# An SSM-and-MLP mix on one core: three parameter rows behind three first blocks, transposes reordered, sine and cosine moved, and no joining block

## The chip, the cores and the metric

The kernel runs on one core of one Trainium2 chip. A core has a matrix engine (PE, whose weight loads are shown as PEld), a vector engine (DVE, VectorE), an activation engine (ACT, ScalarE), a general engine (POOL, GpSimd) and a sequencer for transfers (SP, SyncE). Each runs its own list of instructions in order; semaphores tie the lists together. SP and ACT each have a queue on which they issue transfers (DMAs), and both queues share 16 DMA engines. On-chip memory is SBUF, with 128 partitions; PE writes its results to PSUM, which has eight banks of 512 f32 columns. The metric is the device time in microseconds of one execution.

## The reference

A sequence of 2048 rows of width 448 goes through two branches, and a gate per row mixes them:

```
g = sigmoid((x * gate_w).sum(-1))
dt = exp(log_dt);  Lam = Lambda_re + i Lambda_im;  Lam_bar = exp(dt * Lam)
B_bar = ((Lam_bar - 1) / Lam)[:, None] * (B_re + i B_im)
h[t] = Lam_bar * h[t-1] + B_bar @ x[t]          # complex, 448 states, 2048 steps
a = 2 * Re(h @ C^T) + x * Dskip                 # branch A
b = silu(x @ w1) @ w2                           # branch B, hidden width 1792
out = g * a + (1 - g) * b
```

Inputs and output are bfloat16. For what follows it matters that the complex decay Lam_bar needs, for each state, `exp(dt * Lambda_re)`, and the cosine and the sine of `dt * Lambda_im`; these come from three vectors of 448 numbers: log_dt, Lambda_re, Lambda_im.

## The kernel before

The 2048 rows are cut into even and odd ones and each set into two halves of 512, so x is held transposed in four chunks (XT). Chunk 0 is even, first half. For each chunk, FFN1 (the product with w1, then SiLU) makes 14 blocks of 128 hidden columns, and FFN2 multiplies the result with w2. Branch A multiplies the chunks with B, runs the recurrence on the VectorE as scans in a rotated frame, which needs tables of sine and cosine, and multiplies the states with C at the end.

The width 448 is three slices of 128 (j = 0, 1, 2) and a remainder of 64 (j = 3). Remainders of two blocks, or of two chunks, run at once in the upper and lower 64 rows of PE. For the remainder a copy with the halves swapped, XR, is needed.

All instructions are put into five lists by a small class `Tracker`. `T.op(engine, thunk, reads, writes)` appends an instruction and, ahead of it, the waits that its named buffers ask for: a reader waits for the last writer, a writer for the last writer and all readers. The names are strings; "ps7" is PSUM bank 7. `emit` (lines 139 to 149) writes the lists out, inside `nc.Block()` (line 1178), which gives each engine a block of its own and one joining block behind them, where all engines meet. The order of each list is the order in which the program is written; there is no scheduler.

The start goes like this. SP and ACT issue the loads of x's first chunk (XH), of w1 in pieces, and of four parameter rows into R (log_dt and Lambda_re by SP, Lambda_im and A_Dskip by ACT, line 284; A_Dskip is loaded a second time, for all partitions, by `ld_b`). PE warms up on ones, transposes slices 0 and 1 of chunk 0 into banks 6 and 7 (`turn_x`, line 490; VectorE copies them out in `turned_x`, line 496), and starts the first six FFN1 blocks in banks 0 to 5 (`ffn1_first`, line 430). This function is a generator: it yields at chosen places, and `next(first)` lets it go on to the next one. The last `next` gives the banks. Slices 0 are done in halves of 256 columns, slices 1 and 2 in matmuls of 512.

After slice 1 of two blocks, the rows in R, padded by `rd` (line 463), are turned into columns by four small matmuls (`mm_cols`, line 469), written to bank 7 and copied to PV (line 512). Two more blocks of slice 1 follow, then the transposes of slices 2 and 3 (banks 6 and 7 again), then the last two blocks of slice 1 and all of slice 2. The remainder of the first six blocks (`ffn1_rem`, line 444) closes them in three pairs, each followed by its SiLU evacuation on ScalarE (`ffn1_act`, line 452).

Meanwhile the parameter chain runs on [128 x 4] columns of P: `pts` (line 535) and `ptt` (538) are VectorE instructions, `pact` (541) ScalarE ones. It makes dt, the decay's size mag, the phase as a fraction of a turn (fr), sn and cs (sine and cosine), then lr, li, nli and lis (the products that the scans and the scaling of B's results read) and rr (mag squared). `phases` (lines 587 and 589, on POOL or VectorE) and `phases2` (594) make the angles of the tables, and `swap_xr` (lines 239 and 242) copies XR.

Behind its first loads SP waits for the two pieces of w1's remainder (`T.wait_all("sp", gE)`) and then issues a long row of transposing loads (line 230), the gate and skip vectors, the rest of x, W2, and exchanges of halves between partitions (`swap`, line 937), among them the one of VE that `scan3` reads in its first instruction.

The calls that the change touches are these; the rest of the main program calls generators for FFN1, FFN2, B, the scans and the output one step at a time.

Of the kernel before, what the change touches and what calls it, by code (L numbers as in the profile page):

```python
# [7 lines left out]
ALU = mybir.AluOpType  # L8
# [11 lines left out]
D = 448  # L20
# [22 lines left out]
class Tracker:  # L43
# [92 lines left out]
                self.known[eng][g] = g.total  # L136
                self.ops[eng].append(("wait", g.sem, g.total))

    def emit(self, block):
        where = {"sp": block.sync, "act": block.scalar, "pool": block.gpsimd,  # L140
                 "dve": block.vector, "pe": block.tensor}
        for e in self.ENGINES:
            def body(eng, items=self.ops[e]):
                for it in items:
                    if it[0] == "wait":
                        eng.wait_ge(it[1], it[2])  # L146
                    else:
                        it[1](eng).then_inc(it[2], it[3])
            where[e](body)


def gated_mix(nc, A_x, A_Lambda_re, A_Lambda_im, A_B_re, A_B_im, A_C_re, A_C_im, A_log_dt,
              A_Dskip, B_x, B_w1, B_w2, gate_w, out):
    with ExitStack() as ctx:
        E = ctx.enter_context
        T = Tracker(nc, ctx)

        def sb(name, shape, dtype):
            return E(nc.sbuf_tensor(name, list(shape), dtype))
# [62 lines left out]
        ps = E(nc.psum_tensor("ps", [128, 8, 512], F32))  # L222
# [3 lines left out]
        def ld(eng, dst, src, key, group=None):  # L226
            return T.dma(eng, lambda e: e.dma_start(dst, src), writes=[key], group=group)  # L227
# [17 lines left out]
        T.op("dve", lambda e: e.memset(R[:, :], 0.0), writes=["R0", "R1", "R2", "R3", "Rd"])  # L245
# [16 lines left out]
        def ld_row(eng, i, v):  # L262
            ld(eng, R[i:i + 1, 0:D], row(v), f"R{i}", gR if i < 2 else gR2)
# [17 lines left out]
            ld(eng, XH[:, k, 0:256], x0[:, k, 0:256], XA[k])  # L281
        ld_w("sp", 1)
        ld("act", XH[:, :, 256:512], x0[:, :, 256:512], XA[4])
        for i, (eng, v) in enumerate((("sp", A_log_dt), ("sp", A_Lambda_re), ("act", A_Lambda_im), ("act", A_Dskip))):
            ld_row(eng, i, v)
        ld_w("sp", 2)
        gE = [ld_wr(eng, c, False) for c, eng in enumerate(("sp", "act"))]
# [22 lines left out]
        for i, src in enumerate((A_B_re, A_B_im)):  # L310
# [17 lines left out]
             writes=["IOTA"])  # L328
# [3 lines left out]
        SGN = ["SGa", "SGb"]  # L332
# [91 lines left out]
        def ffn1_first():  # L424
            banks = [nxt() for _ in range(NF1)]
            for j, h in ((0, 0), (0, 1), (1, None), (2, None)):
                c = slice(0, 512) if h is None else slice(256 * h, 256 * h + 256)
                for n, fb in enumerate((0, 2, 4, 1, 3, 5)):
                    bank = banks[fb]
                    T.op("pe", lambda pe, fb=fb, bank=bank, j=j, h=h, c=c: pe.matmul(  # L430
                        ps[:, bank, c], W1E[:, j, ff(fb) * 128:(ff(fb) + 1) * 128], XT[:, j, c],
                        start=(h == 0), stop=(h == 0), skip_group_check=(h != 0)),
                        reads=[f"W1Ej{j}" if j else f"W1Ej0{fb % 2}"] + (
                            ["XTe02"] if j == 2 else [f"XTe0{j}{h}"] if h is not None else [f"XTe0{j}0", f"XTe0{j}1"]),
                        writes=[f"ps{bank}"])
                    if (j, h, n) in ((0, 0, 3), (0, 0, 5), (1, None, 1), (1, None, 3)):
                        yield
            yield banks

        def ffn1_rem(banks, fb):  # L440
            def mm(pe):
                ins = None
                for i, p in enumerate((LO, UP)):
                    ins = pe.matmul(ps[:, banks[fb + i], :], w1(fb + i)(p, 3), xh(0, 0, 3, p), start=False, stop=True,  # L444
                                    skip_group_check=True)
                return ins
            T.op("pe", mm, reads=rem_ffn1(0, 0, fb), writes=[f"ps{banks[fb]}", f"ps{banks[fb + 1]}"])
            ffn1_act(0, fb, banks[fb], 2)
# [11 lines left out]
                yield  # L460

        def rd():
            T.op("dve", lambda e: e.tensor_copy(R[0:4, D:512], R[0:4, 384:448]), reads=["R0", "R1", "R2", "R3"],  # L463
                 writes=["Rd"])

        def mm_cols(pe):
            ins = None
            for pt in range(4):
                ins = pe.matmul(ps[:, 7, pt * 8:pt * 8 + 4], R[:, pt * 128:(pt + 1) * 128],  # L469
                                ID[:, 0:4], start=True, stop=True)  # L470
            return ins
        ones = nc.const_aps.tensor(1.0, [128, 128], BF16)
# [13 lines left out]
        def turn_x(j, i):  # L486
            def mm(pe):
                ins = None
                for k in (2 * i, 2 * i + 1):
                    ins = pe.transpose(xp[j][:, k * 128:(k + 1) * 128], XH[:, k, j * 128:(j + 1) * 128], ID[:, :])  # L490
# [11 lines left out]
        first = ffn1_first()  # L502
# [5 lines left out]
        turned_x(1, 1)  # L508
        rd()
        next(first)  # L510
        T.op("pe", mm_cols, reads=["R0", "R1", "R2", "R3", "Rd", "ID"], writes=["ps7"])
        T.op("dve", lambda e: e.tensor_copy(
            PV[:, :, :], ps[:, 7, 0:32].rearrange("p (t c) -> p t c", c=8)[:, :, 0:4]),
            reads=["ps7"], writes=["PV"])
        next(first)

        names = {}

# [15 lines left out]
        def pts(o, a, s1, s2, op0, op1, ra):  # L534
            T.op("dve", lambda e: e.tensor_scalar(col(o), a, s1, s2, op0, op1), reads=ra, writes=[o])

        def ptt(o, a, b, op, ra):
            T.op("dve", lambda e: e.tensor_tensor(col(o), a, b, op), reads=ra, writes=[o])

        def pact(o, a, f, ra, scale=1.0, bias=0.0):  # L540
            T.op("act", lambda e: e.activation(col(o), a, f, bias=bias, scale=scale),
                 reads=ra, writes=[o])
# [3 lines left out]
            col("phf"), LIM, 1.0 / TWO_PI, col("dt"), ALU.mult, ALU.mult), reads=["PV", "dt"], writes=["phf"])  # L546
        ptt("ar", col("dt"), LRE, ALU.mult, ["dt", "PV"])
        pact("mag", col("ar"), AF.Exp, ["ar"])
        for j in (2, 3):
            for i in range(2):  # L550
                turn_x(j, i)
        for j in (2, 3):
            turned_x(j)
        T.op("dve", lambda e: e.tensor_copy(XR[64:128, 0:512], xp[3][0:64, :]), reads=["ps7"], writes=["XR0a"])
        T.op("act", lambda e: e.activation(JK[:, 0:1], HP[:, :], AF.Silu), reads=["HP"], writes=["JK0"])
        pts("phr", col("phf"), MAGIC, -MAGIC, ALU.add, ALU.add, ["phf"])
# [12 lines left out]
        ptt("li", col("mag"), col("sn"), ALU.mult, ["mag", "sn"])  # L569
        pts("nli", col("li"), -1.0, None, ALU.mult, ALU.bypass, ["li"])  # L570
        T.op("dve", lambda e: e.tensor_tensor(c1("lis", 3), c1("li", 3), SG[:, 0:1], ALU.mult),
             reads=["li"] + SGN, writes=["lis"])
        ptt("rr", col("mag"), col("mag"), ALU.mult, ["mag"])
        first = next(first)


        GP = (0, 0, 1, 1)
# [54 lines left out]
        def skip():  # L632
            for b in range(4):
# [8 lines left out]
        phases(0)  # L642
        phases(2, "dve")
        phases2(0)
        swap_xr("dve", 1, 0)
        phases2(2)
        phases(3)
# [2 lines left out]
             writes=["BTz"] + BTK[2:4])  # L650
# [508 lines left out]
        for _ in range(8):  # L1159
            t = yclose(*yopen())  # L1160
# [14 lines left out]
            yout(2 * kt + odd, bank, c)  # L1175
        T.wait_all("sp", outs)

        with nc.Block() as block:
            T.emit(block)


def bass_gated_mix__ssm_conv_s5__dense_activation_silu__prompt_kernel(nc, *args):
# [29 lines left out]
```

## Time and profile before

| what | before |
|---|---|
| time, median of 3 runs | 139.46 us (139.14 to 139.64) |
| profiled execution: time | 139.14 us |
| profiled execution: span, first to last instruction | 137.0 us (136.99) |
| PE busy | 132.8 us, 97% |
| VectorE busy | 114.7 us, 84% |
| ScalarE busy | 93.7 us, 68% |
| POOL busy | 15.3 us, 11% |
| moved by DMA | 11.94 MB |

The profile lists instructions with their start, their length and, in brackets, how long the engine had been idle before them and what ended that idle time. A time is counted from the first instruction of the program. "x4" means that four instructions of one kind stand in one line. A name like `ps<-XT,W1E` says what is written and from what. SPq and ACTq are the instructions that issue transfers, or wait, without using the engine. Matmuls overlap: one of 512 columns is shown as 0.38 us long, and the next one begins before it ends. The chain that ended last is followed backwards from the last instruction, each time to what released it.

### The profile page before, as it was taken

The numbers are of one execution on the slowest core, as the hardware profiler recorded it, in microseconds if no ns is written. First come the engines' busy times: TensorE is split into PE (matmuls) and PEld (weight loads), VectorE is DVE, ScalarE is ACT, GpSimd is POOL, SyncE is SP. The second block draws the span as 40 slices with busy tenths as digits, with TensorE's granted clock in tenths as the row PEclk, the third lists the DMA queues.
The fourth block names the chain that finished last, engine by engine and source line by source line (L and its number), as shares of the span: only waits on it lengthen the run. The fifth ranks groups of instructions, "written<-read, shape, count | busy, mean of one in ns | idle before, by whom it ended". The sixth has DMA issues, their size and how long they took to land.

```text
span 137.0 us, 2417 instructions
## 1 busy us (share of the span) xinstructions
PE 132.8 (97%) x962; PEld 65.1 (48%) x963; DVE 114.7 (84%) x150; ACT 93.7 (68%) x146; POOL 15.3 (11%) x32
## 2 busy tenths in 40 slices
PE   7889999999999999999999999999999999999992
PEld 7444444444444554444445544445555555555551
DVE  1379999374699999999999999999999999990563
ACT  0369798899939994599997996797214437889200
POOL 7108179305000000000000000000000000000000
PEclk9999999999999999999999999999999999999999
DMA  4998949999999130000320000000000000232123
GB/s 112 264 282 168 170 83 164 146 189 370 384 194 139 36 75 0 5 0 0 77 62 20 0 0 0 5 0 0 0 0 0 0 5 20 80 101 67 67 101 101
DMA packets 24897, 11.94 MB, mean 87 GB/s; under 512 B 16564, under 2 KB 24376, under 8 KB 24888
## 3 DMA queue, kind: packets, MB, share of 16 engines
q1 hardware_dynamic: 23140, 10.76, 35.8%
q10 hardware_dynamic: 1748, 1.04, 2.6%
q8 instruction: 7, 0.11, 0.3%
q14 instruction: 2, 0.02, 0.0%
HBM read 5.51 MB, written 1.84 MB: 54 GB/s over the span
## 4 chain that ended last, share of the span: by engine, by line
PE 91%; DMA 3%; DVE 2%; ACTq 2%; issue 0%; DVEq 0%
PE ps L364 42%; PE ps L772 31%; PE ps L994 15%; DMA R<-in_A_Dskip_dram 3%; ACTq L227 2%; PE ps L430 2%; DVE HS L841 1%; DVE TMPS L1018 1%; PE ps L444 1%; PE ps L490 0%; PE ps L469 0%; DVE R L463 0%; DVEq L146 0%
## 5 line engine op out<-in xcount | busy, mean ns | idle before, releaser
L772 PE MATMUL ps<-W,AT 128*128 128x448 bf16 x224 | 42.9, 353 | 0.0
L364 PE MATMUL ps<-XT,W1E 64*128 64x512 bf16 x325 | 40.1, 376 | 0.0
L452 ACT ACTIVATE AT<-ps 128x1024 bf16<-128x1024 f32 x28 | 28.2, 1019 | 9.9 <-PE ps L364 9.8
L772 PEld LDWEIGHTS ps<-W,AT 128*128 128x128 bf16 x224 | 21.7, 98 | 21.2 <-issue 0.4
L364 PEld LDWEIGHTS ps<-XT,W1E 64*128 64x128 bf16 x325 | 16.5, 94 | 20.0 <-ACT VE L803 0.8
L364 PE MATMUL ps<-XT,BT 64*128 64x512 bf16 x156 | 20.2, 376 | 0.1
L785 ACT ACTIVATE BT<-ps,GT 128x448 bf16<-128x448 f32 x8 | 5.1, 633 | 13.1 <-PE ps L772 13.1
L364 PEld LDWEIGHTS ps<-XT,BT 64*128 64x128 bf16 x156 | 8.1, 94 | 9.6 <-DVE HS L841 0.6
L841 DVE SCALAR_TENSOR_TENSOR HS<-VE,P,ps 128x512 bf16<-128x512 bf16 (+1 forms) x13 | 9.6, 781 | 2.6 <-PE ps L364 2.3
L885 DVE TENSOR_TENSOR_SCAN G<-P,Q 128x1024 f32<-128x1024 f32 (+1 forms) x6 | 11.4, 1921 | 0.0
L994 PE MATMUL ps<-CO,VE 128*128 128x448 bf16 (+2 forms) x63 | 11.1, 332 | 0.0
L994 PE MATMUL ps<-CO,HS 128*128 128x448 bf16 x56 | 11.1, 352 | 0.0
L364 PE MATMUL ps<-XR,W1E 64*128 64x512 bf16 x25 | 9.2, 376 | 0.0
L994 PEld LDWEIGHTS ps<-CO,VE 128*128 128x128 bf16 x63 | 6.0, 98 | 4.8
L994 PEld LDWEIGHTS ps<-CO,HS 128*128 128x128 bf16 x56 | 5.5, 98 | 5.1
L838 DVE TENSOR_TENSOR Q<-G,COS 128x2048 bf16<-128x2048 f32 (+1 forms) x4 | 7.0, 1756 | 0.1
L838 DVE TENSOR_TENSOR Q<-G,SIN 128x2048 bf16<-128x2048 f32 (+1 forms) x4 | 7.0, 1752 | 0.0
L805 ACT ACTIVATE ps<-VE,P 128x1024 f32<-128x1024 bf16 x6 | 6.7, 1119 | 0.2
L841 DVE SCALAR_TENSOR_TENSOR VE<-HS,P,FP 128x512 bf16<-128x512 bf16 (+1 forms) x7 | 6.6, 977 | 0.1
L1018 DVE SCALAR_TENSOR_TENSOR OT<-ps,GT,BT 128x448 bf16<-128x448 f32 x4 | 2.6, 682 | 4.8 <-PE ps L994 4.8
L803 ACT ACTIVATE VE<-ps 128x1024 bf16<-128x1024 f32 x6 | 6.1, 1018 | 0.8 <-PE ps L364 0.8
L841 DVE SCALAR_TENSOR_TENSOR FP<-HS,P,VE 128x1024 f32<-128x1024 bf16 (+1 forms) x4 | 6.2, 1551 | 0.1
(120 smaller groups left out, 170.5 us busy)
## 6 DMA issues: line engine op xcount, KB each, us to landing
W<-in_B_w_dram SPq DMA_DIRECT2D x1, 1568.0 KB, 9.1
XN<-in_A_x_dram SPq DMA_DIRECT2D x1, 896.0 KB, 5.1
out_dram<-OT SPq DMA_DIRECT2D x8, 112.0 KB, 1.7
out_dram<-TMPS SPq DMA_DIRECT2D x7, 112.0 KB, 1.7
HS<-HS SPq DMA_DIRECT2D x4, 128.0 KB, 2.5
W1E<-in_B_w_dram SPq DMA_DIRECT2D x2, 192.0 KB, 4.1
XN<-in_A_x_dram SPq DMA_DIRECT2D x1, 384.0 KB, 5.9
XN<-in_A_x_dram ACTq DMA_DIRECT2D x1, 256.0 KB, 4.6
```

The source lines that it names most:

```text
L227: return T.dma(eng, lambda e: e.dma_start(dst, src), writes=[key], group=group)
L364: ins = pe.matmul(ps[:, bank, :], w(p, j), xh(odd, h, j, p), start=start and j == js[0], stop=stop and j == js[-1], skip_group_check=seeded)
L452: T.op("act", lambda e: e.activation(a[:, fb:fb + n, :], ps[:, bank:bank + n, :], AF.Silu), reads=[f"ps{bank + i}" for i in range(n)], wri ...
L772: ins = pe.matmul(ps[:, bank, 0:D], a[:, fb, q * 128:(q + 1) * 128], W2[:, ff(fb), :], start=(first and fb == 0), stop=(fb == NFB - 1), sk ...
L785: T.op("act", lambda e: e.activation(bs(tile), ps[:, bank, 0:D], AF.Copy, scale=sc), reads=[f"ps{bank}", "GT2" if h else "GRI"], writes=ks)
L803: T.op("act", lambda e: e.activation(VE[:, m:m + 2, hs], ps[:, b[0]:b[0] + 2, :], AF.Copy), reads=[f"ps{i}" for i in b], writes=vs)
L805: T.op("act", lambda e: e.activation(ps[:, o[0]:o[0] + 2, :], VE[:, m:m + 2, hs], AF.Copy, scale=c1("lr", pt)), reads=vs + ["lr"], writes= ...
L838: T.op("dve", lambda e: e.tensor_tensor(o, a, b, op), reads=reads, writes=writes)
L841: T.op("dve", lambda e: e.scalar_tensor_tensor(o, a, s, b, ALU.mult, ALU.add), reads=reads, writes=writes)
L885: T.op("dve", lambda e: e.tensor_tensor_scan(G[:, c, w], rb, Q1[:, c, w], init, ALU.mult, ALU.add), reads=[f"Q1{c}", "rr", f"G{c}"], write ...
L994: ins = pe.matmul(ps[:, bank, c], state(kt, odd, m), CO[:, m, c], start=False, stop=(m == YB[-1]), skip_group_check=True)
L1018: T.op("dve", lambda e: e.scalar_tensor_tensor(o, ps[:, bank, c], g, bs(tile)[:, c], ALU.mult, ALU.add), reads=[f"ps{bank}", "GT1_1", f"BS ...
```

## The change

- `emit` no longer takes a block; the five lists are written straight into the program, and `with nc.Block()` is gone.
- A_Dskip is no longer loaded into R. The columns come from three rows, and the buffer name R3 is gone.
- `ffn1_first` yields after three blocks of slice 1 instead of after two and again after four. The column matmuls come behind these three blocks and write columns 256 to 287 of bank 7 under a name of their own, "pv", instead of the bank's first columns under "ps7". The copy to PV reads both names.
- The transposes of slices 2 and 3 follow directly on PE. VectorE copies slice 2 out at once, slice 3 after the first parameter instructions. The three other blocks of slice 1 and all of slice 2 follow on PE.
- `ffn1_rem` is called earlier in the program, ahead of the tables' angles. Sine and cosine stand between the second and the third of these calls, so on ScalarE they come behind two evacuations. PE's order of these remainders against the rest is the same as before.
- lr, li, nli and lis go into a function `decays`, called after `phases2(0)`; rr is made before the angles.

```diff
-    def emit(self, block):
-        where = {"sp": block.sync, "act": block.scalar, "pool": block.gpsimd,
-                 "dve": block.vector, "pe": block.tensor}
+    def emit(self):
+        nc = self.nc
+        where = {"sp": nc.sync, "act": nc.scalar, "pool": nc.gpsimd, "dve": nc.vector, "pe": nc.tensor}
         for e in self.ENGINES:
...
-        for i, (eng, v) in enumerate((("sp", A_log_dt), ("sp", A_Lambda_re), ("act", A_Lambda_im), ("act", A_Dskip))):
+        for i, (eng, v) in enumerate((("sp", A_log_dt), ("sp", A_Lambda_re), ("act", A_Lambda_im))):
             ld_row(eng, i, v)
...
-                    if (j, h, n) in ((0, 0, 3), (0, 0, 5), (1, None, 1), (1, None, 3)):
+                    if (j, h, n) in ((0, 0, 3), (0, 0, 5), (1, None, 2)):
                         yield
...
-                ins = pe.matmul(ps[:, 7, pt * 8:pt * 8 + 4], R[:, pt * 128:(pt + 1) * 128],
+                ins = pe.matmul(ps[:, 7, 256 + pt * 8:260 + pt * 8], R[:, pt * 128:(pt + 1) * 128],
                                 ID[:, 0:4], start=True, stop=True)
...
         next(first)
-        T.op("pe", mm_cols, reads=["R0", "R1", "R2", "R3", "Rd", "ID"], writes=["ps7"])
+        T.op("pe", mm_cols, reads=["R0", "R1", "R2", "Rd", "ID"], writes=["pv"])
         T.op("dve", lambda e: e.tensor_copy(
-            PV[:, :, :], ps[:, 7, 0:32].rearrange("p (t c) -> p t c", c=8)[:, :, 0:4]),
-            reads=["ps7"], writes=["PV"])
-        next(first)
+            PV[:, :, :], ps[:, 7, 256:288].rearrange("p (t c) -> p t c", c=8)[:, :, 0:4]),
+            reads=["pv", "ps7"], writes=["PV"])
+        for j in (2, 3):
+            for i in range(2):
+                turn_x(j, i)
+        turned_x(2)
...
         pact("mag", col("ar"), AF.Exp, ["ar"])
-        for j in (2, 3):
-            for i in range(2):
-                turn_x(j, i)
-        for j in (2, 3):
-            turned_x(j)
+        turned_x(3)
...
+        first = next(first)
+        ffn1_rem(first, 0)
+        ffn1_rem(first, 2)
         pact("sn", col("fr"), AF.Sin, ["fr"], scale=SIN_SCALE)
         pact("cs", col("afr"), AF.Sin, ["afr", "HP"], scale=-SIN_SCALE, bias=HP[:, 0:1])
-        ptt("lr", col("mag"), col("cs"), ALU.mult, ["mag", "cs"])
...
+        ffn1_rem(first, 4)
+
+        def decays():
+            ptt("lr", col("mag"), col("cs"), ALU.mult, ["mag", "cs"])
+            ptt("li", col("mag"), col("sn"), ALU.mult, ["mag", "sn"])
...
         ptt("rr", col("mag"), col("mag"), ALU.mult, ["mag"])
-        first = next(first)
...
         phases2(0)
+        decays()
         swap_xr("dve", 1, 0)
...
-        for fb in (0, 2, 4):
-            ffn1_rem(first, fb)
         pair(*ffn1_pair(0, NF1))
...
-        with nc.Block() as block:
-            T.emit(block)
+        T.emit()
```

More of the change, by code (lines that the diff above doesn't have):

```diff
@@ L137, in wait_all @@
                 self.ops[eng].append(("wait", g.sem, g.total))
-    def emit(self, block):
-        where = {"sp": block.sync, "act": block.scalar, "pool": block.gpsimd,
-                 "dve": block.vector, "pe": block.tensor}
+    def emit(self):
+        nc = self.nc
+        where = {"sp": nc.sync, "act": nc.scalar, "pool": nc.gpsimd, "dve": nc.vector, "pe": nc.tensor}
         for e in self.ENGINES:
[L143 to L149, printed above, removed]
+            eng = where[e]
+            for it in self.ops[e]:
+                if it[0] == "wait":
+                    eng.wait_ge(it[1], it[2])
+                else:
+                    it[1](eng).then_inc(it[2], it[3])
 def gated_mix(nc, A_x, A_Lambda_re, A_Lambda_im, A_B_re, A_B_im, A_C_re, A_C_im, A_log_dt,
@@ L243, in swap_xr @@
                      writes=[f"XR{h}a"])
-        T.op("dve", lambda e: e.memset(R[:, :], 0.0), writes=["R0", "R1", "R2", "R3", "Rd"])
+        T.op("dve", lambda e: e.memset(R[:, :], 0.0), writes=["R0", "R1", "R2", "Rd"])
         T.op("dve", lambda e: e.memset(SG[0:64, 0:1], -1.0), writes=["SGa"])
@@ L462, in rd @@
         def rd():
-            T.op("dve", lambda e: e.tensor_copy(R[0:4, D:512], R[0:4, 384:448]), reads=["R0", "R1", "R2", "R3"],
+            T.op("dve", lambda e: e.tensor_copy(R[0:3, D:512], R[0:3, 384:448]), reads=["R0", "R1", "R2"],
                  writes=["Rd"])
@@ L565, in gated_mix @@
             reads=["f2"] + SGN, writes=["f2s"])
+        first = next(first)
+        ffn1_rem(first, 0)
+        ffn1_rem(first, 2)
         pact("sn", col("fr"), AF.Sin, ["fr"], scale=SIN_SCALE)
         pact("cs", col("afr"), AF.Sin, ["afr", "HP"], scale=-SIN_SCALE, bias=HP[:, 0:1])
-        ptt("lr", col("mag"), col("cs"), ALU.mult, ["mag", "cs"])
[L569 to L572, printed above, removed]
+        ffn1_rem(first, 4)
+        def decays():
+            ptt("lr", col("mag"), col("cs"), ALU.mult, ["mag", "cs"])
+            ptt("li", col("mag"), col("sn"), ALU.mult, ["mag", "sn"])
+            pts("nli", col("li"), -1.0, None, ALU.mult, ALU.bypass, ["li"])
+            T.op("dve", lambda e: e.tensor_tensor(c1("lis", 3), c1("li", 3), SG[:, 0:1], ALU.mult),
+                 reads=["li"] + SGN, writes=["lis"])
         ptt("rr", col("mag"), col("mag"), ALU.mult, ["mag"])
-        first = next(first)
         GP = (0, 0, 1, 1)
```

## The prediction

> **What bounds the kernel now.** I read the page first, for the engine that is never idle:
>
> ```profile
> PE 132.8 (97%) x962; PEld 65.1 (48%) x963; DVE 114.7 (84%) x150; ACT 93.7 (68%) x146; POOL 15.3 (11%) x32
> PEclk9999999999999999999999999999999999999999
> ```
>
> PE is busy for 132.8 of 137.0 us at full granted clock, so only what makes PE wait, or what lies before its first and after its last matmul, can be gained or lost. The chain that ended last, in order of time, says where:
>
> ```profile
> 3.33 3.44 DMA R<-in_A_Dskip_dram
> ...
> 6.86 0.18 DVE R L463
> ...
> 7.17 0.24 PE ps L469 x4
> ...
> 31.53 1.42 DVE HS L841 x2
> ```
>
> At the front it runs through the fourth parameter row into the column matmuls (line 469); later it is matmuls, but for one turn through VectorE at 31.53. The timeline of 6 to 10.6 us, PE alone, shows the front's steps:
>
> ```profile
> 6.19 0.61 PE L430 MATMUL ps<-XT,W1E 128*128 128x512 bf16 x2 [0.25 <-DMA W1E<-in_B_w_dram]
> 7.17 0.24 PE L469 MATMUL ps<-ID,R 128*128 128x4 bf16 x4 [0.38 <-DVE R L463]
> ...
> 7.71 0.61 PE L490 MATMUL ps<-ID,XN 128*128 128x128 bf16 x8
> 8.15 2.00 PE L430 MATMUL ps<-XT,W1E 128*128 128x512 bf16 x8
> ```
>
> The timeline of 28 to 41.2 us shows a second wait, which the chain does not name because the weight load stands in it. Read it from below: PE waits for VectorE, VectorE for a transfer, and that was issued behind the load of W2:
>
> ```profile
> 29.08 0.50 SPq L227 DMA_DIRECT2D W<-in_B_w_dram  x1
> ...
> 31.57 1.78 SPq L937 DMA_DIRECT2D VE<-VE  x2
> ...
> 39.38 1.28 DVE L841 SCALAR_TENSOR_TENSOR HS<-VE,P,ps 128x1024 bf16<-128x1024 bf16 x1 [0.30 <-DMA VE<-VE]
> ...
> 40.72 0.54 PEld L364 LDWEIGHTS ps<-XT,W1E 64*128 64x128 bf16 x7 [0.49 <-DVE HS L841]
> ```
>
> Last, the rows of line 1178, the end of the joining block, as the answer for that source line gives them (start of each in us):
>
> ```profile
> L1178 SPq COMPARE_BRANCH  x1: 33/33/33, 136.6 to 136.6; - x1
> L1178 SPq DRAIN  x1: 13/13/13, 136.8 to 136.8; - x1
> L1178 SPq EVENT_SEMAPHORE  x1: 17/17/17, 136.9 to 136.9; - x1
> ```
>
> **The change part by part.** *The front.* Pitches first. A 512-column matmul follows the last after 0.215 us (the line-444 ones start at 10.09, 10.31, 10.53), a transpose after 0.056 ((0.61 - 0.22) / 7), and the four column matmuls hold PE 0.10. Before, two blocks go from 6.19 to 6.85 less one pitch, 6.63; then PE stands until 7.17 for the rows. After, three blocks fill PE to 6.85. The column matmuls then wait for the last of three rows. That row's issue starts 0.63 before the dropped one (2.70 against 3.33), so the gain in its landing is between 0 and 0.63; I take 0.2, since both go down one queue behind the same 256 KB of x, and the landings of the two rows on SP are about that far apart in the trace's semaphore records. R is then padded at 6.65 instead of 6.86, and the columns start at 6.97. Four transposes of slice 2 end at 7.29. Slice 3 shares its bank with the columns and waits for the copy to PV: columns' end 7.21, copy 7.25 to 7.43 (0.18, the row of line 512), PE 0.06 later at 7.49. That is a new wait of 0.20, where two blocks and four transposes covered it before. Then 0.22 for slice 3, three blocks (0.645), six blocks (1.29), and 0.10 for the switch to 64-row tiles as at 10.09 now: the first remainder starts at 9.73 instead of 10.09. The wait of 0.12 for slice 2's copy (x8 took 2.00; eight pitches and the pipe give 1.88) is gone, for that copy now runs 7.49 to 7.91 and is wanted at 8.35. Front gain: 0.36 us; with the row's landing at its bounds, 0.16 (nothing earlier) to 0.48 (the columns at 6.85).
>
> [...]
>
> *Sine and cosine behind two evacuations.* ScalarE runs them at 9.88 and 10.17 (0.19 + 0.30) and its first evacuation at 10.52. After, evacuations 1 and 2 run at about 10.16 and 11.12, the two small ones cost 0.3 to 0.45, and evacuation 3 ends near 13.5 instead of 13.4. PE asks for its banks (4 and 5) at 14.2 at the earliest (now about 14.6, less 0.36). Cover 0.7 us, cost 0. Evacuation 1 itself ends 0.36 earlier, as PE wants it (PE follows it at 11.61 now with 0.07 to spare). Queued behind is only ScalarE's next evacuation.
>
> *The four decay products on VectorE* move behind phases2(0). They cost 0.15 to 0.16 each (one took 0.92 beside POOL's work); their readers are the ScalarE scaling at 26.47 and POOL's coefficients after 19.24. VectorE would be done near 15.3. Cost 0; its next, the swap of XR (now 16.05), comes no later, since the long phase instructions start a microsecond sooner, and PE reads XR for this half at 18.52.
>
> *Queues.* ACT's queue loses one issue of 0.24; its four later W1 loads are issued that much sooner, but land behind the same x block. SP's queue is passed by nothing. POOL's phases start 0.4 sooner, hidden either way.
>
> *What becomes of the 0.36.* At 31.53 VectorE had been idle for 0.45, so that turn follows PE. At 40.72 it does not: the instruction at 39.38 starts when the exchange of VE lands, 6.6 to 7.0 us after its issue, while the four equally large HS exchanges take a median of 2.5. It sits behind W2, issued at 29.08 and landed 9.1 later, at 38.2. Both hang on SP's row of transposes, which starts at 7.88 behind W1's remainder rows and waits for no engine. PE at 40.72 is already 0.16 late against its pitch (last pair 40.35, next due 40.56). So the front gain is lost there, but for what SP's queue itself moves: 0 if the queue keeps its times, 0.36 if it ran away with PE. I take 0.1, near the lower end, since one row less leaves the same megabytes before it.
>
> *The joining block.* Last branch 136.6, drain 136.8, release 136.9, end of span 137.0. With the block gone the last wait on the output transfers, 0.03 long, ends the span: 0.35 less. No row shows a branch at the start, so 0 there. Whether the 2.15 us outside the span (139.14 - 136.99) change is not shown; between the whole 0.35 given back and 0.15 more (other engines early at what follows), I take 0, as nothing outside was edited. [...]
>
> Sum: 0.10 + 0.35 = 0.45 us. The profiled execution took 139.14 (span 136.99); it would take 138.69. The median of the runs is 139.46, so 139.0.
>
> **The rivals.** *A, the front gain arrives:* the VE exchange lands 0.3 earlier because SP's transposes start earlier. For it: W1's loads share engines at 280 GB/s with the rows. Against: 9.1 us of W2 lie between. 0.36 + 0.35: 138.75. *B, the join moves into what follows the span:* the engines must still be gathered, the 0.35 come back outside it; 0.1 remains: 139.35. Against: other engines are idle by then already. *C, slower:* ACT's earlier W1 loads push SP's remainder rows and with them every transpose and W2. Every 0.1 that the VE exchange lands later is 0.1 at PE, for there is no slack at 40.72; the place is 39.38. With the end's 0.35 kept, it is slower than now from 0.35 of delay, and by 0.3% from 0.77. A transpose issue under load took 4.33 (19.33) and a like one later 2.10 (25.00), so a microsecond can come: 139.46 - 0.35 + 0.9 = 140.0. Against: the shift is one issue of 0.24.
>
> **How the numbers follow.** 0.3% is 0.42 us, about what a measurement here can tell from no change. My case 0.55 (138.75 to 139.25, somewhat over half of it below 139.04), A 0.15, B 0.18, C 0.08, other 0.04. Faster by over 0.3%: 0.32 + 0.15 + 0.02 = 0.49; slower 0.08; within 0.43. The range runs from A with the 0.15 outside, 138.6, to B with the measured spread of 0.2 on top, 139.55.
>
> **What would show it.** Column matmuls near 7.0 with three blocks ahead; a PE gap of 0.2 before slice 3; the first remainder at 9.7; the wait for VE<-VE grown from 0.30 to about 0.55, and PE at the line-364 load after it near 40.6; no row of the joining block and the span ending 0.1 behind the last output's landing. I am wrong if PE stands at 40.4 or earlier there (A), if the span shrinks and the time does not (B), or if 39.38 has become later (C).

## The result and the profile after

| what | before | after |
|---|---|---|
| time, median of 8 runs each, same chip | 139.34 us (139.06 to 139.93) | 138.38 us (137.86 to 139.26) |
| ratio, with its 95% interval | | 0.993 [0.9902, 0.9959] |
| profiled execution: time | 139.14 us | 138.07 us |
| profiled execution: span | 136.99 us | 136.55 us |
| profiled execution: time less span | 2.15 us | 1.52 us |

Medians and ranges in this document leave out executions more than 1.5% above the fastest of their kernel: below, one of the block alone (140.65), one of W2 in halves (142.40) and a few of the kernel before.

The change is faster by 0.96 us in the medians, about 0.7%. The forecast was 139.0 with a range from 138.6, so the time lies below the range, and the direction was right. In the profiled executions 1.07 us went: 0.44 inside the span and 0.63 outside it. The forecast had 0.45 inside and nothing outside. Of the time less the span, the eight runs of after have a median of 1.49. The kernel before has 1.99 in the 51 runs that the experiments made of it, from 1.69 to 2.17; so the 2.15 of its profiled execution is near the top, and about 0.5 of the 0.63 is the change.

PE's share on the page of after, answering the first line shown of before:

```profile
PE 133.4 (98%) x962; PEld 65.7 (48%) x963; DVE 113.9 (83%) x150; ACT 93.5 (69%) x146; POOL 16.9 (12%) x32
```

PE is busy 0.6 us more than before with the same 962 matmuls; the last part of this text says where. The chain that ended last, for the kernel after and in order of time (start, length, what):

```profile
7.35 0.24 PE ps L468 x4
...
10.96 20.52 PE ps L363 x190
...
31.58 1.42 DVE HS L846 x2
...
33.05 10.00 PE ps L363 x90
...
134.03 0.90 DVE TMPS L1023 x2
```

The column matmuls (now line 468) stand at 7.35, later than the 7.17 of before, and the turn through VectorE at 31.58 instead of 31.53. The timeline of PE from 6 to 10.6 us shows the new order (the first line's matmuls reach into the three blocks):

```profile
5.67 1.62 PE L429 MATMUL ps<-XT,W1E 128*128 128x256 bf16 x9
7.35 0.24 PE L468 MATMUL ps<-ID,R 128*128 128x4 bf16 x4
7.45 0.81 PE L489 MATMUL ps<-ID,XN 128*128 128x128 bf16 x8
8.31 1.89 PE L429 MATMUL ps<-XT,W1E 128*128 128x512 bf16 x8
10.13 0.39 PE L443 MATMUL ps<-XT,W1E 64*128 64x512 bf16 x1
```

Three blocks, the columns, eight transposes, then eight blocks in 1.89 without the wait of 0.12 that stood in them before: the order did what the diff says. But the first remainder (line 443) starts at 10.13, against 9.73 in the forecast and 10.09 before:

```profile
10.09 0.39 PE L444 MATMUL ps<-XT,W1E 64*128 64x512 bf16 x1
```

The reason is one line of the timeline of VectorE, the padding of R with the rows:

```profile
7.04 0.17 DVE L462 COPY R<-R 3x64 bf16<-3x64 bf16 x1 [0.83 <-DMA R<-in_A_Lambda_im_dram]
```

It waited for Lambda_im's row, and runs at 7.04 where before, with four rows, it ran at 6.86. By the trace's semaphore records the last row landed at 6.95 (before: 6.78).

The timeline of 28 to 41.2 us, with the exchange behind W2:

```profile
29.09 0.51 SPq L226 DMA_DIRECT2D W<-in_B_w_dram  x1
...
31.62 1.83 SPq L942 DMA_DIRECT2D VE<-VE  x2
...
39.37 1.28 DVE L846 SCALAR_TENSOR_TENSOR HS<-VE,P,ps 128x1024 bf16<-128x1024 bf16 x1 [0.24 <-DMA VE<-VE]
...
40.70 0.54 PEld L363 LDWEIGHTS ps<-XT,W1E 64*128 64x128 bf16 x7 [0.43 <-DVE HS L846]
```

VectorE at 39.37 (39.38 before) and PE at 40.70 (40.72): from there the two traces run within 0.02 us of each other to the last matmul, 134.27 against 134.28. So nothing between the first and the last matmul contributed. What is left inside the span is the end. No row of the joining block is there; SP's waits by source line end with the one at 136.5, and it closes the span:

```profile
L146 SPq EVENT_SEMAPHORE  x11: 17/28/28, 7.7 to 136.5; - x11
```

What lies behind the span is not on the page, but the trace keeps semaphore records. A semaphore that the program doesn't use, number 2, is raised nine times right behind the program, and nine times more 0.79 us after that, in every profile of this case. The first round, in us of the span's clock:

```
before  137.26 137.29 137.47 137.52 137.54 137.64 137.68 137.71 137.76   (span ends 136.99)
after   134.68 135.60 135.64 135.68 136.69 136.74 136.78 136.81 136.86   (span ends 136.55)
```

Before, all nine come after the span, the last 0.77 behind it. After, four of them have come while SP still waits for the output, and the last is 0.31 behind. That is 0.46 of the 0.63 saved outside; most of the rest is the high 2.15 of before. The last four steps of after take 0.17 in all, or 43 ns each.

### The profile page after: what moved, and what is told of

Read it like the earlier page. It is cut to its first block, busy times and chain, and to the rows that moved or that the text cites. A ratio compares the mean times of both kernels' runs of the same rounds, so it can differ in the third digit from the quotient of the medians.

```text
span 136.6 us, 2406 instructions
## 1 busy us (share of the span) xinstructions
PE 133.4 (98%) x962; PEld 65.7 (48%) x963; DVE 113.9 (83%) x150; ACT 93.5 (69%) x146; POOL 16.9 (12%) x32
## 3 DMA queue, kind: packets, MB, share of 16 engines
q10 hardware_dynamic: 1746, 1.04, 2.6%
## 4 chain that ended last, share of the span: by engine, by line
PE 96%; DVE 2%; issue 0%; DVEq 0%
PE ps L363 43%; PE ps L777 31%; PE ps L999 15%; PE ps L429 3%; PE ps L477 2%; PE ps L489 1%; DVE HS L846 1%; DVE TMPS L1023 1%; PE ps L443 1%; PE ps L468 0%; DVEq L146 0%
```

## The experiments

The theories at the start. *The block:* nearly all of the gain is the joining block, in the span's end and in what follows. *The front:* the reorder at the start gives a part that the single profile didn't catch, or is swallowed at 40.7 by the exchange behind W2; if the exchange is taken out of W2's way it must come through. Later a third question came up: whether the gain outside the span is the block's instructions being gone, or the other engines being done early.

A calculation helps in reading all of them: the span, less the start of the first remainder, is all that follows the front.

**The block alone** (the kernel before, written out without it):

```diff
...
-        with nc.Block() as block:
-            T.emit(block)
+        T.emit()
```

> The kernel before, with the joining block alone taken out. Theory J (all of the measured 0.96 us is the join: 0.35 inside the span, 0.6 in what the engines do after it, because the others are already waiting there when SP comes): 138.4, that is 0.9 to 1.0 below the kernel before, span about 0.35 shorter, time minus span about 1.5 instead of 2.15. Rival F (the front brings a good part): 138.9 to 139.0, 0.35 to 0.45 below. Rival B of the prediction (the join comes back outside): within 0.1 of before.

Measured: median 138.45 (138.0 to 139.87), the kernel before on the same chip 139.35; ratio 0.9932 [0.9901, 0.9962]. The median of the time less the span is 1.52. The profile has a span of 136.48, the first remainder at 10.05 and the exchange landed at 39.27. With the ratio of the whole change at 0.993, the block alone gives nearly everything: 0.90 of 0.96.

**All but the block** (the kernel after, with it):

```diff
...
-        T.emit()
+        with nc.Block() as block:
+            T.emit(block)
```

> The changed kernel with the joining block put back. Theory J: as the kernel before, within 0.15 us, time minus span 2.15. Rival F: 0.4 to 0.6 us below the kernel before, from the reordered front.

Measured: median 138.95 (138.65 to 140.17), ratio 0.9987 [0.996, 1.0013], so no difference that the measurement can tell; time less span 2.04. The two halves agree as far as they can: with the block gone, the rest of the change adds nothing that shows (0.993 against 0.9932); with the block kept, the median lies 0.40 below that of the kernel before, the ratio says 0.18, and its interval reaches from 0.56 lower to 0.18 higher. A gain of some tenths from the rest of the change is not excluded by it.

Its profile even shows such a gain: a span of 136.67, 0.31 less than before, with the first remainder at 9.95. In the timeline of 28 to 42.2 us W2 and the exchange are early:

```profile
27.86 0.51 SPq L227 DMA_DIRECT2D W<-in_B_w_dram  x1
...
31.43 1.68 SPq L943 DMA_DIRECT2D VE<-VE  x2
```

The exchange landed at 39.05, and VectorE did not wait for it. So with W2 whole, too, a front gain can pass, when the exchange happens to land early enough.

**Why the time behind the span shrinks.** The kernel after, without the block, but with every engine waiting for the last two output transfers:

```diff
         T.wait_all("sp", outs)
+        for e in ("act", "pool", "dve", "pe"):
+            T.wait_all(e, outs[-2:])
```

> The changed kernel, still without the joining block, but ACT, POOL, VectorE and PE also wait at their ends for the last two output transfers, as SP does. Theory W (what lies outside the span got shorter because the four others are through it before SP comes): time minus span goes back from 1.5 to about 1.9 to 2.0, the span stays without the 0.35; 138.8. Rival I (the block's own instructions, its branches and drains, cost the 0.6): time minus span stays at 1.5, 138.4.

Measured: median 138.79 (138.6 to 139.51), ratio 0.9969 [0.9944, 0.9994]. The time less the span has a median of 2.02, as with the block (2.04) and not as without (1.49 to 1.53). There is no block in this kernel, so what costs 0.5 us there is not its instructions, it is that all engines reach the end together. Its records of semaphore 2 show the same: 137.01 to 137.63, all nine behind the span's end at 136.82.

This run gave more than it was made for, since in its profile the rows landed early, the last at 6.37. PE's timeline:

```profile
6.94 0.24 PE L468 MATMUL ps<-ID,R 128*128 128x4 bf16 x4
...
9.72 0.39 PE L443 MATMUL ps<-XT,W1E 64*128 64x512 bf16 x1
```

The first remainder is at 9.72, where the forecast had 9.73. In part that is luck: R was padded from 6.39, and it was the third block that set the columns at 6.94, not the rows, as the forecast had it. And this is what became of it (timeline of 28 to 42.2 us):

```profile
28.04 0.51 SPq L226 DMA_DIRECT2D W<-in_B_w_dram  x1
...
31.21 2.11 SPq L942 DMA_DIRECT2D VE<-VE  x2
...
39.61 1.28 DVE L846 SCALAR_TENSOR_TENSOR HS<-VE,P,ps 128x1024 bf16<-128x1024 bf16 x1 [0.87 <-DMA VE<-VE]
...
40.95 1.03 PE L363 MATMUL ps<-XT,W1E 64*128 64x512 bf16 x7 [0.58 <-DVE HS L846]
```

The exchange, although issued sooner, landed at 39.59, VectorE stood for 0.87, and the span less the first remainder is 127.10, against 126.42 of after (136.55 - 10.13). Against after, the front came 0.41 early and 0.68 went again.

**W2 in two halves, the second behind the exchange** (on the kernel after; FFN2 waits for both):

```diff
-        def load_w2():
-            ld("sp", W2[:, :, :], B_w2.rearrange("(f p) d -> p f d", p=128), "W2")
+        def load_w2(i):
+            ld("sp", W2[:, 7 * i:7 * i + 7, :],
+               B_w2[896 * i:896 * i + 896, :].rearrange("(f p) d -> p f d", p=128), f"W2{i}")
...
-        load_w2()
+        load_w2(0)
...
         bu_odd(0, 0)
+        load_w2(1)
```

> The changed kernel with W2 loaded in two halves, the second issued behind the exchange of VE, so that the exchange no longer waits for all of W2. Theory G (PE at 40.7 is gated by that exchange): the exchange lands near 36 to 37 instead of 39.36, the wait of 0.16 against PE's pitch at 40.7 is gone, and with it what the front wins in a given execution: 0.15 to 0.5 us below the changed kernel (137.9 to 138.2 against 138.4). Rival: another gate (the odd x transposes at 28 us, or the scan's next instruction) takes over at once, and it is within 0.1 of the changed kernel. If the second half of W2 comes too late for FFN2 at 43 us, it is slower.

Measured: median 137.83 (137.63 to 138.42), ratio 0.9873 [0.9829, 0.9917], the best of the first four. Its timeline of 28 to 42.2 us shows the second half behind the exchange:

```profile
27.92 1.02 SPq L226 DMA_DIRECT2D W<-in_B_w_dram  x1
...
31.72 1.17 SPq L943 DMA_DIRECT2D VE<-VE  x2
...
32.94 0.60 SPq L226 DMA_DIRECT2D W<-in_B_w_dram  x1
```

The rows of the tile VE, 30 to 42.2 us, then say how long the exchange took (in us, where before and after had 6.5 to 7.0):

```profile
DMA to landing us min/median/max: 4.0/4.1/4.1
```

It lands at 36.31 (in the seven other profiles with W2 in halves at 37.3 to 38.6). The waits of 30 to 42.2 us hold no VE<-VE any more; of the two turns only the one that follows PE is left:

```profile
DVE HS L847 <- PE ps L363: 2.5, 2, 1.9
...
PEld ps L363 <- DVE HS L847: 0.6, 1, 0.6
```

The same list of after has the wait that is gone: 

```profile
DVE HS L846 <- DMA VE<-VE: 0.2, 1, 0.2
```

**The old front with W2 in two halves** (on the kernel before, without the block):

```diff
...
-        with nc.Block() as block:
-            T.emit(block)
+        T.emit()
...
-        load_w2()
+        load_w2(0)
...
         bu_odd(0, 0)
+        load_w2(1)
```

> The kernel before without the joining block and with W2 in two halves; against e3 it has the old front alone. Theory G with a front gain of 0.36: 0.3 to 0.4 us slower than e3, and 0.15 below e1. If the front gains nothing even when it is let through, it equals e3 within 0.1.

Measured: median 138.43 (137.86 to 138.86), ratio 0.9915 [0.9885, 0.9945]; the exchange landed at 38.63 and PE didn't wait. So the four medians without a block are: old front 138.45 with W2 whole and 138.43 split, new front 138.38 and 137.83. The split by itself does little, the new front by itself does little, both together 0.6. That looks like a gate at 40.7, but it isn't evidence for one. The median spans are 136.9, 136.7, 136.85 and 136.6, without such a pattern: of the 0.6 between the two split kernels 0.42 lies outside the span (median of the time less the span 1.70 against 1.28), where a gate inside can do nothing. The intervals of their ratios, [0.9829, 0.9917] and [0.9885, 0.9945], overlap, and their profiles (first remainder at 10.26 and 10.23) differ by 0.03 only. What settles it are the profiles in the table below.

**The changed kernel once more, and W2 in halves beside it, on one chip.** To see the spread, the kernel after was run again with no edit, and the split with it:

> The changed kernel itself, as the control for the three that follow on the same chip: 138.4. Its profile shows the exchange of VE landing near 39.3 to 39.6 and PE's wait at 40.7, larger the earlier its front was.

> e3 again beside the control. Theory G (the exchange behind W2 holds back what the front wins): 0.4 to 0.6 below the control, no wait at 40.7. Rival (e3's 137.85 was chance, with five runs): within 0.2 of the control.

Measured: after 138.06 (137.71 to 139.18), ratio 0.987 [0.9832, 0.9908] against the kernel before, which took 139.88 on this chip; the split 137.83 (137.33 to 138.16), ratio 0.9852 [0.9817, 0.9887]. The two can't be told apart by their medians. But the control's profiled execution is its slowest, 139.18 with a span of 137.59, and shows why. Its timeline from 28 to 42.2 us:

```profile
31.64 2.47 SPq L942 DMA_DIRECT2D VE<-VE  x2
...
40.42 1.28 DVE L846 SCALAR_TENSOR_TENSOR HS<-VE,P,ps 128x1024 bf16<-128x1024 bf16 x1 [1.26 <-DMA VE<-VE]
...
41.76 0.82 PE L363 MATMUL ps<-XT,W1E 64*128 64x512 bf16 x5 [0.96 <-DVE HS L846]
```

and its chain, which now names the exchange:

```profile
33.52 6.87 DMA VE<-VE
40.42 1.29 DVE HS L846
41.76 2.33 PE ps L363 x20
...
135.08 0.90 DVE TMPS L1023 x2
```

The same kernel, the exchange landed at 40.39 instead of 39.35: 1.04 later; the span 137.59 instead of 136.55: 1.04 longer. The split's profile on this chip had the exchange at 38.07 and no wait. Between these two profiles with W2 whole, the delay of that landing is paid in full.

**Four variants of the front, all with W2 in halves**, to see which term of the front is worth what. The fourth row back in R:

```diff
-        for i, (eng, v) in enumerate((("sp", A_log_dt), ("sp", A_Lambda_re), ("act", A_Lambda_im))):
+        for i, (eng, v) in enumerate((("sp", A_log_dt), ("sp", A_Lambda_re), ("act", A_Lambda_im), ("act", A_Dskip))):
...
```

> e3 (changed kernel, W2 in halves) with the fourth row loaded into R again, as before. If the prediction's row term holds, the columns start 0.2 us later against the last W1 load of slice 1 and the time is 0.2 above e3 (138.05). Rival (the last row lands with the 256 KB of x in front of it, however many rows there are): within 0.1 of e3.

Measured: median 138.2 (137.55 to 138.55), ratio 0.9923 [0.9891, 0.9955]. The rows landed at 7.07 with four, 7.06 with three in the split kernel, and the first remainder started at 10.25 against 10.23. The dropped row is worth nothing that shows: over all profiles the last row landed at 6.55 to 7.07 with four rows (four profiles) and, where Lambda_im's row stands behind the block of x, at 6.37 to 7.08 with three (eight profiles). The median is 0.37 above that of W2 in halves (137.83), even more than the 0.2 of the expectation, but not for its reason: the median spans are both 136.6, and the difference lies in the time outside them (1.66 against 1.28).

One block of slice 1 moved between the transposes of slices 2 and 3, to cover the new wait of 0.2:

```diff
-                    if (j, h, n) in ((0, 0, 3), (0, 0, 5), (1, None, 2)):
+                    if (j, h, n) in ((0, 0, 3), (0, 0, 5), (1, None, 2), (1, None, 3)):
...
-        for j in (2, 3):
-            for i in range(2):
-                turn_x(j, i)
-        turned_x(2)
+        for i in range(2):
+            turn_x(2, i)
+        turned_x(2)
+        next(first)
+        for i in range(2):
+            turn_x(3, i)
```

> e3 with one of the three later blocks of slice 1 put between the transposes of slice 2 and those of slice 3, so that it covers the copy to PV. If the new wait of 0.19 before slice 3 is real PE time: 0.15 to 0.2 below e3 (137.65 to 137.7), and the gap before slice 3 is gone from the trace. If it is hidden elsewhere: as e3.

Measured: median 137.87 (137.19 to 138.29), ratio 0.9894 [0.9857, 0.9931]; profiled span 136.17. PE's timeline from 3.95 to 10.5 us:

```profile
7.25 0.24 PE L468 MATMUL ps<-ID,R 128*128 128x4 bf16 x4
7.35 0.38 PE L489 MATMUL ps<-ID,XN 128*128 128x128 bf16 x4
7.57 0.38 PE L429 MATMUL ps<-XT,W1E 128*128 128x512 bf16 x1
7.79 0.39 PE L489 MATMUL ps<-ID,XN 128*128 128x128 bf16 x4
...
9.83 0.39 PE L443 MATMUL ps<-XT,W1E 64*128 64x512 bf16 x1
```

From the columns to the first remainder it takes 2.58, where after, with the wait, took 2.78 (10.13 - 7.35). So the new wait does cost 0.20, and it is gone with one block in its place.

The row of Lambda_im ahead of the block of x on ScalarE's queue:

```diff
-        ld("act", XH[:, :, 256:512], x0[:, :, 256:512], XA[4])
         for i, (eng, v) in enumerate((("sp", A_log_dt), ("sp", A_Lambda_re), ("act", A_Lambda_im))):
             ld_row(eng, i, v)
+        ld("act", XH[:, :, 256:512], x0[:, :, 256:512], XA[4])
```

> e3 with ACT's parameter row issued ahead of its 256 KB of x instead of behind. If the rows' landing (6.8 to 7.1 in the profiles) is what the front waits for: R is padded near 6.2 instead of 7.0, the columns follow the third block without a wait, the first remainder starts 0.2 to 0.4 earlier, and the time is 0.2 to 0.4 below e3. Rival: the same transfers in another order only move the wait to the x block (slice 2's transposes) or to W1's slice 1, within 0.1 of e3.

Measured: median 137.93 (137.29 to 138.44), ratio 0.9897 [0.9862, 0.9932]; profiled execution 137.29, span 135.69. That row landed at 4.3, and R was padded at 6.27 in place of 7.14. In the timelines of VectorE and PE the rows still set the columns, but now it is SP's row of Lambda_re, landed at 6.24; the third block, which began at 6.24, would have let them start at about 6.46 by the pitch of 0.215:

```profile
6.27 0.17 DVE L462 COPY R<-R 3x64 bf16<-3x64 bf16 x1 [0.86 <-DMA R<-in_A_Lambda_re_dram]
...
6.58 0.24 PE L468 MATMUL ps<-ID,R 128*128 128x4 bf16 x4
...
9.36 0.39 PE L443 MATMUL ps<-XT,W1E 64*128 64x512 bf16 x1
```

What held ScalarE's row up is the block of x ahead of it on the queue (it landed at 7.06 behind that block in the split kernel, at 4.3 ahead of it here), not the row behind it. The rival came true in small: slice 2's transposes then waited 0.1 for the block of x, which landed at 6.73. Both edits together:

```diff
...
+        next(first)
+        for i in range(2):
+            turn_x(3, i)
...
             ld_row(eng, i, v)
+        ld("act", XH[:, :, 256:512], x0[:, :, 256:512], XA[4])
```

> e3 with both the row first and the block as cover: if the two front waits add, 0.3 to 0.5 below e10 (137.4); if the front is bound by W1's slice 1 in most executions, 0.1 below or equal.

Measured: median 137.70 (137.28 to 138.17), ratio 0.9848 [0.981, 0.9886]; profiled span 136.01, row at 3.96, first remainder at 9.69. It has the lowest median of all, and its interval doesn't separate it from the plain split on the same chip (0.9852). Its front is later than with the row alone (9.69 against 9.36), since the piece of W1 for slice 1 landed at 6.40 instead of 5.75 and the three blocks waited for it; R had been padded at 6.00. That is the second of the two expectations, in one profile.

The medians of these four don't order them. Their profiles do:

| kernel | first remainder | exchange landed | span | difference |
|---|---|---|---|---|
| W2 in halves | 10.23 | 36.31 | 136.56 | 126.33 |
| the same, second chip | 10.33 | 38.07 | 136.67 | 126.34 |
| old front, W2 in halves | 10.26 | 38.63 | 136.60 | 126.34 |
| one block as cover | 9.83 | 38.27 | 136.17 | 126.34 |
| Lambda_im's row first | 9.36 | 37.34 | 135.69 | 126.33 |
| row first and cover | 9.69 | 37.27 | 136.01 | 126.32 |
| after | 10.13 | 39.35 | 136.55 | 126.42 |
| before without the block | 10.05 | 39.27 | 136.48 | 126.43 |
| every engine waits | 9.72 | 39.59 | 136.82 | 127.10 |
| after, second chip | 10.16 | 40.39 | 137.59 | 127.43 |

"Difference" is the span less the start of the first remainder. In the six rows with the second half of W2 behind the exchange it is 126.32 to 126.34, whatever the front does: a front that is 0.87 earlier gives a span that is 0.87 shorter. In the four with W2 whole it is larger by as much as the exchange is late: the landing less the first remainder is 29.22, 29.22, 29.87 and 30.23, and the difference exceeds 126.33 by 0.09, 0.10, 0.77 and 1.10: in each about as much as the former exceeds 29.13. The two profiles with the joining block fit as well, if the start of the last matmul stands for the end of the span: it comes 124.02 or 124.03 behind the first remainder with W2 in halves, 124.19 in before (landing less first remainder 29.27) and 124.03 in all but the block (29.10, no wait). So the gate is shown, in twelve executions, by one rule; the fourth row back and sine and cosine early, with 126.33 and 126.32, are two more.

**Sine and cosine back in front of the evacuations**, with W2 in halves:

```diff
-        pact("sn", col("fr"), AF.Sin, ["fr"], scale=SIN_SCALE)
-        pact("cs", col("afr"), AF.Sin, ["afr", "HP"], scale=-SIN_SCALE, bias=HP[:, 0:1])
...
+        pact("sn", col("fr"), AF.Sin, ["fr"], scale=SIN_SCALE)
+        pact("cs", col("afr"), AF.Sin, ["afr", "HP"], scale=-SIN_SCALE, bias=HP[:, 0:1])
         first = next(first)
```

> e3 with sine and cosine ahead of the three evacuations again. The prediction gave their move a cost of 0 either way: within 0.1 of e10. Rival: they stand in the way of the first evacuation (now that the front is earlier, PE follows it with 0.07 to spare), 0.1 to 0.4 above e10.

Measured: median 138.1 (137.64 to 138.39), ratio 0.9869 [0.9831, 0.9908], beside 137.83 (137.33 to 138.16) of the split on the same chip. The ranges overlap for most of their length, and the profiled span less the first remainder is 126.32 (136.58 - 10.26) as in the table. So the place of the two costs nothing inside the span that the profile shows. The 0.27 between the medians lies mostly outside the span too (median of the time less the span 1.75 against 1.43, median span 136.45 against 136.3); why is open.

## Why the prediction was off

The step that failed is the one on what lies outside the span: "I take 0, as nothing outside was edited". It had a bound of "0.15 more (other engines early at what follows)". The mechanism in that bound was the right one, and it was mis-sized: 0.63 in the profiled execution, and 0.5 between kernels whose engines meet at the end and those whose engines don't (1.99, 2.02 and 2.04 against 1.49, 1.52 and 1.53). No row of before prices what follows the span; its semaphore records do show nine raises 0.27 to 0.77 behind it, but the prediction didn't draw on them there. With 0.5 instead of 0 the sum would have been 0.95, where 0.96 was measured. That the 0.45 inside the span agrees with the 0.44 measured is in part luck: the joining block was worth 0.08 more than forecast and the front 0.09 less. The 0.35 for the block was an estimate of the span's end alone. The block also kept the other four engines from going early through what follows the program: of the first round of semaphore 2 four raises came at 134.68 to 135.68 in after, none ahead of 137.26 in before. This was worth more, 0.5 against 0.43. The first round ends 0.77 behind the span with the block and 0.31 without.

*The joining block inside the span*: forecast 0.35, measured 0.43 (0.44 less span, of which 0.01 is PE). Right. Rival B, the join moving into what follows the span, is refuted: what follows became shorter, 1.49 against 1.99 in the medians.

*The front*: forecast 0.36 earlier, measured 0.04 later in the profile of after. Its terms, one by one. The columns to the first remainder: forecast 2.76 (9.73 - 6.97), measured 2.78 or 2.79 in after, in the run where every engine waits, and with the row first (the forecast's own terms add up to 9.75 rather than 9.73). The new wait before slice 3: forecast 0.20, and the run with a block as cover got back 0.20. The lost wait in the eight blocks: 2.00 became 1.89, as forecast. Only the row's landing failed: 0.2 earlier was taken, from bounds of 0 to 0.63, and it came 0.17 later; with the fourth row put back it moved by 0.01, and the landings with three and with four rows cover the same range. The reordering itself is then the rest: from the last row's landing to the first remainder it takes 3.18 with the new front in four profiles where the rows set the columns (after, its repetition, all but the block, W2 in halves), against 3.31 with the old front in two (before, old front with W2 in halves; 3.50 in the third, where W1 came late). That is 0.13, against 0.16 in the forecast.

*The loss at 40.72*: the forecast let only 0.1 of the front through. In the result there was no front gain to lose, so that says nothing of it; the experiments show the gate. With W2 whole, a front 0.41 early was lost in the run where every engine waits; with W2 in halves, all of it arrives. Rival A needed the exchange to land earlier with the front, and it doesn't follow: issued 0.41 sooner in the run where every engine waits (31.21 against 31.62), it landed 0.24 later; issued 0.14 sooner than before in all but the block, it landed 0.31 earlier, and there the front gain arrived as in A. Rival C's mechanism exists, since the control's exchange landed 1.04 later and cost 1.04; but it is a spread between executions of one kernel, and nothing shows that the change brought it.

*Sine, cosine, decays, queues*: 0 was forecast and nothing contradicts it. ScalarE's third evacuation ends at 13.7 (13.5 in the forecast) before PE wants its banks, and the first evacuation that follows PE again starts at 14.88 instead of 14.83. The decays on VectorE took until 16.1 instead of the 15.3 forecast, since one of them took 0.9 beside POOL's work, which delayed the copy of XR to 16.15 from 16.05; PE reads it at 18.5.

Two things stay open: why the last row lands anywhere from 6.4 to 7.1 in profiles of kernels that issue it alike, and why the time less the span of the kernels with W2 in halves is about 1.25 in some runs and about 1.7 in others, while their records of semaphore 2 look alike. Until the second is known, the medians of those kernels say little about differences of a few tenths.

## What to carry to other kernels

Where a kernel ends, let each engine end as soon as its own work is done and let only one wait for the last transfer: here a join at the end cost 0.43 us inside the span and 0.5 behind it, and the second part is visible in no busy row. Before a gain at the front is counted, look for the transfer that later work meets at a fixed time; here an exchange queued behind the load of W2 could take back the whole gain (0.41 early at the front, 0.68 lost behind it), and with half of W2 behind it each gain of the front arrived in the span, one for one (span less front 126.32 to 126.34). With a spread of about a microsecond between executions of one kernel, a difference of two rows of one profile (span less front) tells variants apart that the medians can't.

## What was not expected of the hardware

The first is the one above: engines that are done early go through what follows the program early. In after four of the nine raises of semaphore 2 came by 135.68, ahead of the end of the span at 136.55; before, and where every engine waits, all nine came behind it, and the time less the span has a median of 1.99 and 2.02 there, against 1.49.

The second is in the first matmuls of the front. The timeline of PE from 3.95 us, four matmuls of 256 columns, first of before and then of after:

```profile
4.01 0.60 PE L430 MATMUL ps<-XT,W1E 128*128 128x256 bf16 x4
```

```profile
4.01 1.01 PE L429 MATMUL ps<-XT,W1E 128*128 128x256 bf16 x4
```

In after they follow each other at about 0.21 us until near 6 us, in before at about 0.11, although the profile's row of the granted clock shows 9 in each slice of both. The blocks at the slow pitch fill the time in which PE stood before, and this is most likely the 0.6 of additional busy time of PE: over all profiles PE is busy for 132.6 to 132.8 in the four at the fast pitch, one of them with the new order (all but the block), and for 133.0 to 133.6 in the eight whose first four matmuls ran at the slow one. No run tries it by itself. It is not a property of the change: the slow pitch stands in the profiles of some kernels without regard to their edits (the kernel after twice, W2 in halves twice, sine and cosine early) and not in others (before, before without the block, all but the block, Lambda_im's row first). In after it is hidden, as the rows come later than the blocks end (columns at 7.35, third block done at about 7.13). In W2 in halves on the second chip it is not: the columns follow the third block at 7.54, though R was padded from 7.09. What decides it no run here shows.

The third is how much a place on a queue counts for a small transfer: the single row of Lambda_im landed at 6.1 to 7.1 us behind the block of x, and at 4.0 to 4.3 ahead of it.
